# Pooling the second batch's keys: uncast pixels, row sums by GpSimd, two chunks per job, and three more GELU chunks for VectorE

## The chip, the cores and the metric

The kernel runs on one core of one Trainium2 chip. The metric is the time of one execution on the device in microseconds (us), the median of three runs. The profile is one execution taken by the hardware profiler; its times are counted from the start of its span.

## What is computed

Attention over pooled keys, followed by a feed-forward layer with a quick GELU. There are 4 batches of 12288 queries with 128 channels, 49152 rows in all; the keys are a 384 x 32 image of 128 channels per batch, pooled 4 x 4 to 768 keys.

```python
# q (4, 12288, 128), kv (4, 384, 32, 128), w_sr (128, 128)
kv_pool = kv.reshape(B, H // 4, 4, W // 4, 4, C).mean(axis=(2, 4))
k = v = kv_pool.reshape(B, -1, C) @ w_sr
s = (q @ k.transpose(0, 2, 1)) / sqrt(C)
x = softmax(s) @ v                       # (49152, 128)
h = x @ w_in                             # w_in (128, 2048)
out = (h / (1 + exp(-1.702 * h))) @ w_out
```

## The kernel before, in words

**Stages.** The rows are cut into 96 groups of 512 (`NG`), 24 to a batch. Work is done in two rounds of 48 groups (`R = 2`): attention for a round, then the feed-forward layer for it. The unit is a chunk: 512 rows against 128 keys (six to a group, `JC`) or against 128 of the 2048 hidden channels (16 to a group, `FCH`). A fill is TensorE's first matmul of up to three chunks into three of the eight PSUM banks (`fill_attn` L337, `fill_moe` L584), followed by one ScalarE activation of 128x1536 that reads them and writes weights to the buffer `ag`, which has room for 102 chunks. Two sets of three banks take turns; the other two banks are for everything else (`acc`). A drain is the second matmul, from `ag`: four of 129 columns for each attention chunk (`drain_attn` L344), one of 512 for each feed-forward chunk (`drain_moe` L590). After an attention drain VectorE divides by the sums and writes rows to `x` (L376, L379). These are put away in HBM (`put_away` L489) and brought back transposed (`bring_back` L496), as the first matmul of the feed-forward layer wants them. After a feed-forward drain VectorE transposes the group's result (L607), and SyncE's queue writes it out.

**The order.** There is no scheduler at run time. A planner at the end of the kernel (L783 to L851) walks through the fills, and between two of them puts drains, small jobs (`extras`) and steps for VectorE, by a model of the time in units of one 512-column matmul. `FIXED` and `CHUNK` are the model of an activation, `COST` and `COPY` that of the small jobs, and `RECIPROCAL` that of a reciprocal of 128x256 on VectorE. What comes out is one fixed row of instructions per engine, which the engines run in order, held up only by semaphores. `background(i)` (L517) starts loads and small jobs when the fill of group i is placed.

**The keys.** Batch 0 and batch 1 use `load_chunk` (L126): one DMA of GpSimd's queue reads 128 rows of 16 pixels as fp32 and writes them as bf16 into a slice of `x` that is free then. `pool_chunk` (L133) sums with TensorE: for each of four windows, four matmuls with the stationary operand a pixel row block and the moving operand `sum4` (128x32), accumulated over the four pixels, 16 matmuls in all, and one copy by VectorE. `key_and_value` (L157) then makes keys and values of the chunk with two matmuls of 128 columns and two copies. For batch 1 the loads are started at groups 10 and 12, three each; pooling and keys run at groups 15 to 20 and 16 to 21. Group 24 is the first that needs batch 1's keys. Batches 2 and 3 are pooled by accumulating DMAs (`add_kv` L168) and are not touched here.

**The queries.** `cast_q` (L207) writes a slice of four groups to HBM as bf16 (GpSimd's queue), and `load_qT` (L212) brings it back transposed on SyncE's queue. `CAST` and `TURN` say at which group.

**Gates.** GpSimd's and SyncE's queues would run far ahead. `gate` (L506) has VectorE write one element, and GpSimd write it again, so that GpSimd's next DMA is held until VectorE has come that far. For SyncE a write into the target by VectorE does the same (L214).

**Chunks made by VectorE.** Some exponentials (`rolling`, `early`) and 14 GELU chunks (`lent` L322: the last chunk of every third group from 52 on) are computed by VectorE instead of ScalarE, in a row of elementwise steps (`early_exp` L416, `lent_gelu` L438). The result goes to `aside`, which has room for three.

Of the kernel before, what the change touches and what calls it, by code (L numbers as in the profile page):

```python
# [24 lines left out]
def kernel(  # L25
    ctx, tc, q, kv, w_sr, moe_w_in, moe_w_out, out,
):
    nc = tc.nc
    B, N, C = q.shape
    _, H, W, _ = kv.shape  # L30
    r = 4
# [101 lines left out]
    def pool_chunk(b, jc):  # L133
# [7 lines left out]
        pTs[b, jc] = kvtmp.tile([128, 128], BF, name="pTc", bufs=2)  # L141
        nc.vector.tensor_copy(pTs[b, jc], ps[:, 0:128])

    def key_chunk(b, jc):
# [10 lines left out]
        vs[b, jc] = True  # L155

    def key_and_value(b, jc):  # L157
        if (b, jc) == (1, 0):
            new_keys(b)
        ps = acc()  # L160
        nc.tensor.matmul(ps[:, 0:128], w_sr_sb, pTs[b, jc], start=True, stop=True)
        nc.tensor.matmul(ps[:, 128:256], pTs.pop((b, jc)), w_sr_sb, start=True, stop=True)
# [156 lines left out]

    early = range(NG // R, NG // R + EARLY)  # L320
    rolling = [(i, JC - 1) for i in [*range(38, NG // R, 6), *range(57, 90, 6)]]
    lent = [(g, FCH - 1) for g in range(52, 94, 3)]  # L322
    aside = agpool.tile([128, K, 512], BF, name="aside")

    def weights(c):
# [161 lines left out]
    PART, FIRST = 24, 3  # L487

    def put_away(n, m):  # L489
        size = PART // 2 if n == 0 and m > FIRST else PART  # L490
        for o in range(m * PART, m * PART + PART, size):
            lo = n * XS * SG + o * T
            nc.sync.dma_start(out=x_bf[lo:lo + size * T, :].rearrange("(k p) c -> p k c", p=T),
                              in_=x[:, o * T:(o + size) * T].rearrange("p (k c) -> p k c", k=size))
# [11 lines left out]
    def gate():  # L506

        one = gate_tile[:, gates[0] % 8:gates[0] % 8 + 1]
        gates[0] += 1
        nc.vector.memset(one, 0.0)  # L510
        nc.gpsimd.memset(one, 0.0)  # L511

    TURN = {6: 3, 7: 4, 8: 5, 20: 6, 21: 7, 22: 8, 30: 9, 32: 10, 35: 11, 40: 12}
    CAST = {0: [5], 13: [6], 14: [7], 15: [8], 25: [9, 10], 26: [11, 12]}
    CAST_MOE = {20: 13, 21: 14, 22: 15, 23: 16, 33: 17, 34: 18, 35: 19, 36: 20, 37: 21, 38: 22, 39: 23}

    def background(i):  # L517

        first_round = i < GB * 2
        s = TURN.get(i, NS) if first_round else i // 4 + 3 if i % 4 == 0 else NS  # L520
        if s < NS:
            load_qT(s)
        if i in CAST:
            gate()
            for s in CAST[i]:
                cast_q(s)
        if i in (10, 12):
            gate()
            for jc in range(i % 10 * 3 // 2, i % 10 * 3 // 2 + 3):
# [9 lines left out]
        if i == 27:  # L539
            gate()  # L540
            nc.gpsimd.dma_start(out=w_in_sb, in_=moe_w_in)
        if i == 28:
            gate()
            nc.gpsimd.dma_start(out=w_out_sb, in_=moe_w_out.rearrange("(o p) c -> p o c", p=128))

# [155 lines left out]
    def prepare(p):  # L701

        nonlocal now
        kind, part = seq[p]
        for i, jc in part:
            if (kind, i) not in begun:
                begun.add((kind, i))
                (background if kind == "a" else background_moe)(i)
            while kind == "a" and ((key_and_value, i // GB, jc) in extras or (transpose_q, i) in extras):
# [24 lines left out]


    FIXED, CHUNK, SWITCH, HANDOVER, EVACUATE = 0.295, 1.978, 6.0, 1.0, 4.5
    COST = {pool_chunk: (1.9, 2.6), key_chunk: (0.3, 2.4), value_chunk: (0.3, 2.4),
            transpose_q: (1.05, 4.2), early_fill: (1.0, 5.5), key_and_value: (0.55, 3.5),
            transpose_pooled: (0.9, 3.6), make_k: (0.8, 3.2), make_v: (0.8, 3.7)}
    COPY = {pool_chunk: 1.5, key_chunk: 1.5, value_chunk: 1.5, key_and_value: 2.8, transpose_q: 3.2}  # L740
    SMALL = 0.26
    RECIPROCAL = 10.5
    PAUSE = 4.0
    end, extra_at = [], 0.0
    source, dve = None, 0.0
# [137 lines left out]
```

The softmax here doesn't subtract the row's maximum and nothing guards it: scores larger than these inputs give would overflow.

## Time and profile before

The time is 951.16 us (950.90 to 951.42); the profiled execution has a span of 949.0 us.

| engine | busy us | share of the span | instructions |
|---|---|---|---|
| TensorE matmul (PE) | 941.5 | 99% | 6314 |
| VectorE (DVE) | 536.8 | 57% | 1037 |
| ScalarE (ACT) | 933.9 | 98% | 708 |
| GpSimd (POOL) | 67.0 | 7% | 115 |

The costliest groups of instructions, by line:

| line | what | times | busy us | mean ns |
|---|---|---|---|---|
| L588 | ACT, GELU of three chunks | 510 | 682.2 | 1507 |
| L586 | PE, feed-forward fill, 512 columns | 1522 | 411.7 | 379 |
| L596 | PE, feed-forward drain, 512 columns | 1506 | 407.8 | 379 |
| L342 | ACT, exponential of three chunks | 192 | 245.8 | 1439 |
| L353 | PE, attention drain, 129 columns | 2272 | 163.7 | 220 |
| L340 | PE, attention fill, 512 columns | 544 | 148.7 | 379 |
| L139 | PE, pooling, 32 columns (batches 0 and 1) | 192 | small | 177 |
| L463 | DVE, half a reciprocal of a GELU chunk | 28 | 47.6 | 1726 |

How to read it: a matmul's 379 ns is its own way through the array; the next one starts long before it ends, so means do not add up to the span, and how closely starts follow each other tells more. The stages, from the windows: attention of the first round up to about 142 us, feed-forward to 487, attention of the second round to 604, feed-forward to the end. L139, L161 and L162 name the pooling and key matmuls of both batch 0 (up to 25 us) and batch 1 (from 52.8 us on).

### The profile page before, as it was taken

Reading aid. Unit: us, or ns where it says so; the run is one execution under the profiler, and the core shown is the slowest. Engines: PE = TensorE matmul, PEld = TensorE weight load, DVE = VectorE, ACT = ScalarE, POOL = GpSimd, SP = SyncE. Lnnn points to the kernel's source line nnn. Section 1 sums busy time; section 2 is a strip of 40 time slices with the busy share of each in tenths; the row PEclk is TensorE's granted clock in tenths of the full one; section 3 lists DMA queues with packets and bytes.
Section 4 is the critical chain, followed back from the end, with each engine's and each line's share of the span. In section 5 each row is a group of like instructions: output and inputs, shape, how many; then the busy total and the mean of one; then the engine's idle time right before and its main releaser. Section 6 shows DMA issues by size and latency. Waiting matters only on the chain.

```text
span 949.0 us, 15424 instructions
## 1 busy us (share of the span) xinstructions
PE 941.5 (99%) x6314; PEld 503.1 (53%) x6314; DVE 536.8 (57%) x1037; ACT 933.9 (98%) x708; POOL 67.0 (7%) x115
## 2 busy tenths in 40 slices
PE   8999999999999999999999999999999999999998
PEld 4677776444444444454446777754444444444444
DVE  5643553102477777778655765365666665566631
ACT  5999999999999999999999999999999999999998
POOL 4101001330000232000000000000000000000000
PEclk9999999999999999999999999999999999999999
DMA  9999922999867799865335583552222222222222
GB/s 182 203 181 193 214 57 42 157 127 170 162 132 113 116 147 125 123 103 78 65 55 112 133 160 77 134 122 35 44 34 45 34 46 34 45 33 45 34 45 45
DMA packets 372871, 94.93 MB, mean 100 GB/s; under 512 B 346736, under 2 KB 370416, under 8 KB 372464
## 3 DMA queue, kind: packets, MB, share of 16 engines
q1 hardware_dynamic: 343872, 61.31, 36.5%
q0 software_dynamic: 28656, 32.51, 22.6%
q8 instruction: 49, 0.80, 0.4%
q14 instruction: 22, 0.18, 0.1%
q10 hardware_dynamic: 272, 0.13, 0.0%
HBM read 52.49 MB, written 48.76 MB: 107 GB/s over the span
## 4 chain that ended last, share of the span: by engine, by line
ACT 88%; PE 9%; DMA 2%; issue 0%; DVE 0%; POOL 0%; POOLq 0%
ACT ag L588 71%; ACT ag L342 17%; PE banks L340 4%; PE banks L353 3%; DMA x<-in_kv_dram 1%; DMA qT<-q_bf 1%; PE banks L139 0%; PE banks L586 0%; PE banks L624 0%; ACT L588 0%; PE banks L596 0%; PE banks L233 0%; ACT L342 0%; DVE kT L163 0%; POOL x L222 0%
## 5 line engine op out<-in xcount | busy, mean ns | idle before, releaser
L588 ACT ACTIVATE ag<-banks 128x1536 bf16<-128x1536 f32 (+1 forms) x510 | 682.2, 1507 | 0.0
L586 PE MATMUL banks<-x,w_in_sb 128*128 128x512 bf16 x1522 | 411.7, 379 | 0.1
L596 PE MATMUL banks<-ag,w_out_sb 128*128 128x512 bf16 x1506 | 407.8, 379 | 0.0
L342 ACT ACTIVATE ag<-banks 128x1536 bf16<-128x1536 f32 (+2 forms) x192 | 245.8, 1439 | 3.7 <-PE banks L340 3.3
L596 PEld LDWEIGHTS <-w_out_sb 128*128 128x128 bf16 x1520 | 148.5, 98 | 178.0 <-issue 0.9
L586 PEld LDWEIGHTS <-w_in_sb 128*128 128x128 bf16 x1522 | 147.3, 98 | 170.4 <-issue 1.1
L607 DVE STREAM_TRANSPOSE o_sb<-banks 128x512 f32<-128x512 f32 x95 | 67.9, 715 | 210.7 <-PE banks L596 199.9
L353 PEld LDWEIGHTS <-ag 128*128 128x128 bf16 x2272 | 146.1, 98 | 46.4 <-issue 0.6
L353 PE MATMUL banks<-v,ag 128*128 128x129 bf16 x2272 | 163.7, 220 | 0.1
L340 PE MATMUL banks<-qT,kT 128*128 128x512 bf16 x544 | 148.7, 379 | 1.6 <-DVE kT L163 1.0
L432 DVE SCALAR_TENSOR_TENSOR ea<-ea,eb 128x512 f32<-128x512 f32 x128 | 87.8, 686 | 3.2
L376 DVE RECIPROCAL rec<-banks 128x3 f32<-128x3 f32 x124 | 22.2, 179 | 96.0 <-PE banks L353 96.0
L379 DVE TENSOR_TENSOR x<-banks,rec 128x384 bf16<-128x384 f32 x124 | 69.1, 557 | 4.3
L340 PEld LDWEIGHTS <-kT 128*128 128x128 bf16 x544 | 46.3, 98 | 26.6 <-DVE kT L163 1.7
L463 DVE RECIPROCAL eb<-ea 128x256 f32<-128x256 f32 x28 | 47.6, 1726 | 0.5
L173 POOL DMA_DIRECT2D kvs<-in_kv_dram x32 | 40.4, 1315 | 20.8 <-DMA kvs<-in_kv_dram 17.8
L421 DVE TENSOR_SCALAR ea<-banks 128x512 f32<-128x512 f32 x32 | 22.1, 692 | 32.6 <-PE banks L405 32.4
L456 DVE SCALAR_TENSOR_TENSOR ea<-ea,eb 128x512 f32<-128x512 f32 x56 | 38.3, 685 | 1.6
L511 POOL MEMSET gate_tile<- 1x1 f32 x37 | 3.9, 105 | 323.1 <-DVE gate_tile L510 323.1
L427 DVE SCALAR_TENSOR_TENSOR eb<-eb,ea 128x512 f32<-128x512 f32 x32 | 22.1, 690 | 0.9
L443 DVE TENSOR_SCALAR qT<-banks 128x512 f32<-128x512 f32 x14 | 9.7, 692 | 17.2 <-PE banks L399 16.9
L434 DVE SCALAR_TENSOR_TENSOR ag<-ea,ee 128x512 bf16<-128x512 f32 x24 | 16.5, 688 | 0.7
(84 smaller groups left out, 267.6 us busy)
## 6 DMA issues: line engine op xcount, KB each, us to landing
out_dram<-o_sb SPq DMA_DIRECT2D x380, 64.0 KB, 2.0
kvs<-in_kv_dram POOLq DMA_DIRECT2D x32, 384.0 KB, 6.5
q_bf<-in_q_dram POOLq DMA_DIRECT2D x21, 512.0 KB, 6.9
x_bf<-x SPq DMA_DIRECT2D x12, 768.0 KB, 5.8
x<-in_kv_dram POOLq DMA_DIRECT2D x12, 512.0 KB, 10.5
x_bf<-x SPq DMA_DIRECT2D x8, 384.0 KB, 4.5
x<-in_q_dram POOLq DMA_DIRECT2D x5, 256.0 KB, 15.2
w_in_sb<-in_moe_w_in_dram POOLq DMA_DIRECT2D x1, 512.0 KB, 9.6
```

The costliest lines, as they stand in the source:

```text
L173: nc.gpsimd.dma_start(out=kv_sums[b][:, i2], in_=kv_p[b, i, w, :, i2], **({"accum_op": ADD} if n else {}))
L340: nc.tensor.matmul(ps[:, k, :], kTs[i // GB][:, jc * 128:(jc + 1) * 128], rhs, start=True, stop=True)
L342: nc.scalar.activation(place([("a",) + c for c in chunks]), ps, AF.Exp, scale=scale)
L353: nc.tensor.matmul(av_of[u][:, k * (C + 1):(k + 1) * (C + 1)], weights(("a", i, jc))[:, o:o + T], vs[i // GB][:, jc, 0:C + 1], start=(jc = ...
L379: nc.vector.tensor_tensor(to, ps[:, :, 0:C], rec.unsqueeze(2).broadcast_to([128, TS, C]), MUL)
L432: nc.vector.scalar_tensor_tensor(a, a, COEFFS[k], b, ADD, MUL)
L456: nc.vector.scalar_tensor_tensor(a, a, COEFFS[k], b, ADD, MUL)
L463: nc.vector.reciprocal(b[:, m:m + 256], a[:, m:m + 256])
L586: nc.tensor.matmul(ps[:, k, :], w_in_sb[:, fc * 128:(fc + 1) * 128], x[:, g % (4 * XS) * G:(g % (4 * XS) + 1) * G], start=True, stop=True)
L588: nc.scalar.activation(place([("m",) + c for c in chunks]), ps, AF.Gelu_apprx_sigmoid)
L596: nc.tensor.matmul(o_of[g], w_out_sb[:, fc, :], weights(("m", g, fc)), start=(fc == 0), stop=(fc == FCH - 1))
L607: nc.vector.transpose(o_sb, o_of.pop(g))
```

## The change

Batch 1's pixels are no longer cast on the way. `load_pixels` loads one chunk at a time on SyncE's queue as fp32, twice the room in SBUF, so that three chunks fit and the fourth waits for the first to be summed. GpSimd, which has little to do, adds the four pixels of a window in three `tensor_tensor` instructions per chunk (`sum_pixels`); the third writes bf16 into half of a buffer from the pool of the output tiles. TensorE then needs one matmul per window instead of four, and two chunks are one job (`pool_sums`, `key_pair`): eight matmuls of 32 columns and one copy, then one matmul of 256 columns, two of 128, and two copies. It is meant to take matmuls and copies away and to give the idle engine work.

With it come: 17 GELU chunks for VectorE instead of 14 (the last chunk of groups 52, 54, 57, 59 and so on); casts and loads of the queries moved (slices 6 to 8 are cast three groups later, behind most of GpSimd's adds; slices 9 to 12 and the weights one group earlier); two more blocks of `x` put away in halves; two gates fewer on GpSimd's queue, while only the first three of the six loads on SyncE's queue have a holding write; and planner costs for the new jobs, with 8.2 instead of 10.5 for a reciprocal.

```diff
+    def load_pixels(jc):
+        a, ch = divmod(jc, HC)
+        o = (XS - JC) * SG + jc % 3 * 2 * SG
+        t = x[:, o:o + 2 * SG].bitcast(F32)
+        if jc < 3:
+            nc.vector.memset(t[:, 0:1], 0.0)
+        nc.sync.dma_start(out=t, in_=kv_r[1, a, ch])
+        kv_tiles[1, jc] = t.rearrange("p (wp w1 c) -> p w1 wp c", w1=r, c=C)
+    def sum_pixels(jc):
+        t = kv_tiles.pop((1, jc))
+        if jc % 2 == 0:
+            held[jc // 2] = opool.tile([128, 512], F32, name="o_sb").bitcast(BF)
+        sums[jc] = held[jc // 2][:, jc % 2 * 512:jc % 2 * 512 + 512].rearrange("p (wp c) -> p wp c", c=C)
+        nc.gpsimd.tensor_tensor(t[:, 0], t[:, 0], t[:, 1], ADD)
+        nc.gpsimd.tensor_tensor(t[:, 2], t[:, 2], t[:, 3], ADD)
+        nc.gpsimd.tensor_tensor(sums[jc], t[:, 0], t[:, 2], ADD)
+    def pool_sums(b, jc):
+        ps = acc()
+        for k in range(2):
+            for wp in range(4):
+                o = k * 128 + 32 * wp
+                nc.tensor.matmul(ps[:, o:o + 32], sums[jc + k][:, wp, :], sum4, start=True, stop=True)
+        pTs[b, jc] = kvtmp.tile([128, 256], BF, name="pTp")
+        nc.vector.tensor_copy(pTs[b, jc], ps[:, 0:256])
+    def key_pair(b, jc):
...
+        nc.tensor.matmul(ps[:, 0:256], w_sr_sb, pT, start=True, stop=True)
+        for k in range(2):
+            nc.tensor.matmul(ps[:, 256 + k * 128:384 + k * 128], pT[:, k * 128:(k + 1) * 128], w_sr_sb,
+                             start=True, stop=True)
+        nc.vector.tensor_copy(kTs[b][:, jc * 128:(jc + 2) * 128], ps[:, 0:256])
+        nc.vector.tensor_copy(vs[b][:, jc:jc + 2, 0:C], ps[:, 256:512].rearrange("p (k c) -> p k c", k=2))
...
-    lent = [(g, FCH - 1) for g in range(52, 94, 3)]
+    lent = [(g, FCH - 1) for g in range(52, 94) if g % 5 in (2, 4)]
...
-        size = PART // 2 if n == 0 and m > FIRST else PART
+        size = PART // 2 if n == 0 and m > 1 else PART
...
-    TURN = {6: 3, 7: 4, 8: 5, 20: 6, 21: 7, 22: 8, 30: 9, 32: 10, 35: 11, 40: 12}
-    CAST = {0: [5], 13: [6], 14: [7], 15: [8], 25: [9, 10], 26: [11, 12]}
+    TURN = {6: 3, 7: 4, 8: 5, 20: 6, 21: 7, 22: 8, 29: 9, 31: 10, 35: 11, 40: 12}
+    CAST = {0: [5], 16: [6], 17: [7], 18: [8], 24: [9, 10], 25: [11, 12]}
...
-        if i in (10, 12):
-            gate()
-            for jc in range(i % 10 * 3 // 2, i % 10 * 3 // 2 + 3):
-                load_chunk(1, jc)
-        if 0 <= i - 16 < JC:
-            extras.append((key_and_value, 1, i - 16))
-        if 0 <= i - 15 < JC:
-            extras.append((pool_chunk, 1, i - 15))
+        if 10 <= i < 10 + JC:
+            if i > 10:
+                sum_pixels(i - 11)
+            for jc in range(3) if i == 10 else [i - 8] if i < 14 and i > 10 else []:
+                load_pixels(jc)
+        if i == 10 + JC:
+            sum_pixels(JC - 1)
+        if i in (15, 18, 21):
+            extras.append((pool_sums, 1, (i - 15) // 3 * 2))
+        if i in (16, 19, 22):
+            extras.append((key_pair, 1, (i - 16) // 3 * 2))
...
-    RECIPROCAL = 10.5
+    RECIPROCAL = 8.2
```

More of the change, by code (lines that the diff above doesn't have):

```diff
@@ L142, in pool_chunk @@
         nc.vector.tensor_copy(pTs[b, jc], ps[:, 0:128])
+    held, sums = {}, {}
+    def load_pixels(jc):
[23 more added lines that the diff above has]
+    def key_pair(b, jc):
+        if jc == 0:
+            new_keys(b)
+        ps = acc()
+        pT = pTs.pop((b, jc))
+        nc.tensor.matmul(ps[:, 0:256], w_sr_sb, pT, start=True, stop=True)
[4 more added lines that the diff above has]
+        nc.vector.tensor_copy(vs[b][:, jc:jc + 2, 0:C], ps[:, 256:512].rearrange("p (k c) -> p k c", k=2))
+        vs[b, jc] = vs[b, jc + 1] = True
     def key_chunk(b, jc):
@@ L157, in key_and_value @@
     def key_and_value(b, jc):
-        if (b, jc) == (1, 0):
-            new_keys(b)
         ps = acc()
@@ L538, in background @@
             bring_back(0, (i - 31) // 5)
-        if i == 27:
+        if i == 26:
             gate()
             nc.gpsimd.dma_start(out=w_in_sb, in_=moe_w_in)
-        if i == 28:
+        if i == 27:
             gate()
@@ L708, in prepare @@
                 (background if kind == "a" else background_moe)(i)
-            while kind == "a" and ((key_and_value, i // GB, jc) in extras or (transpose_q, i) in extras):
+            while kind == "a" and ((key_pair, i // GB, jc // 2 * 2) in extras or (transpose_q, i) in extras):
                 f, *args = extras.pop(0)
@@ L736 @@
     FIXED, CHUNK, SWITCH, HANDOVER, EVACUATE = 0.295, 1.978, 6.0, 1.0, 4.5
-    COST = {pool_chunk: (1.9, 2.6), key_chunk: (0.3, 2.4), value_chunk: (0.3, 2.4),
+    COST = {pool_chunk: (1.9, 2.6), pool_sums: (1.1, 3.2), key_pair: (1.1, 5.0), key_chunk: (0.3, 2.4), value_chunk: (0.3, 2.4),
             transpose_q: (1.05, 4.2), early_fill: (1.0, 5.5), key_and_value: (0.55, 3.5),
             transpose_pooled: (0.9, 3.6), make_k: (0.8, 3.2), make_v: (0.8, 3.7)}
-    COPY = {pool_chunk: 1.5, key_chunk: 1.5, value_chunk: 1.5, key_and_value: 2.8, transpose_q: 3.2}
+    COPY = {pool_chunk: 1.5, pool_sums: 2.1, key_pair: 4.2, key_chunk: 1.5, value_chunk: 1.5, key_and_value: 2.8, transpose_q: 3.2}
     SMALL = 0.26
-    RECIPROCAL = 10.5
+    RECIPROCAL = 8.2
     PAUSE = 4.0
```

## The prediction

> **What bounds the kernel now.** I read the page first, its chain of waits next, then the windows and the timeline.
>
> ```profile
> PE 941.5 (99%) x6314; PEld 503.1 (53%) x6314; DVE 536.8 (57%) x1037; ACT 933.9 (98%) x708; POOL 67.0 (7%) x115
> ...
> ACT 88%; PE 9%; DMA 2%; issue 0%; DVE 0%; POOL 0%; POOLq 0%
> ```
>
> TensorE (PE) and ScalarE (ACT) are both full, and the chain names ACT. Since each hands work to the other all the time, the chain can walk back through either. So I ask each engine for its smallest pitch. First PE, by windows:
>
> ```profile
> core 0: us, PE busy (x) PEld busy (x) DVE busy (x) ACT busy (x) POOL busy (x), PEclk, DMA share, GB/s
> 45.00:75.00 30.00, 29.90 (x394) 21.91 (x392) 12.84 (x49) 29.89 (x23) 3.34 (x9) 1.00 0.94 177
> 160.00:260.00 100.00, 100.00 (x481) 45.89 (x479) 21.61 (x44) 100.00 (x75) 19.13 (x21) 1.00 1.00 149
> 660.00:900.00 240.00, 240.00 (x1113) 108.77 (x1112) 148.89 (x209) 240.00 (x179) 0.00 (x0) 1.00 0.25 39
> ```
>
> From 660 to 900 us, 1113 matmuls, all 512 columns wide, take 240 us: 215.6 ns each. The timeline has three of them start 0.65 us before the next three (660.18, 660.82), 215 ns each. That is the pitch of matmuls in one unbroken row, so PE has no hole there. Now ACT, in the end of the first attention stage:
>
> ```profile
> 128.66 13.60 ACT L342 ACTIVATE ag<-banks 128x1536 bf16<-128x1536 f32 x10
> ```
> ```profile
> 139.31 2.95 ACT L342 ACTIVATE ag<-banks 128x1536 bf16<-128x1536 f32 x2
> ```
>
> The ninth starts 10.65 us after the first: 1.331 us a piece, the floor of a 1536-wide activation (its mean of 1507 ns includes overlap with the one before). The chain has ACT L588 x28 in 37.6 us from 885.5 to 923.2, a pitch of 1.345. So late in the run PE runs at its floor and ACT 1% above its own. PE is the narrower one. Added up by kind from the program's order, at 216 ns (512 columns), 57 (129), 56 (128) and 25 (32), PE's work is 933 us of 949; most of the rest lies before 40 us. ACT from 13.1 us, at its floor of 1.331 (0.90 for 1024), needs 921 us and takes 931.
>
> **What the skill says.** Perfetto Trace Analysis, "Identifying the Most-Contended Engine", calls matmul busy time a poor measure, since matmuls are pipelined: the trace agrees (a row of 379 ns every 216), which is why I use pitches. TensorE: Matmul & The Clock Gate, "Back-to-back issue gap", gives N/2.4 + 2.5 ns, 215.8 for 512 columns, and about 25 ns up to 64 columns: the trace shows 215.6 and 25. It also says that 512-column streams sustain 131 ns; no such pitch stands here, and the measurement decides. SBUF, "two separate sides", says that GpSimd and VectorE share a port pair, locked when VectorE has two SBUF inputs or a two-port mode; in 46 to 69 us VectorE's long work (L379, the copies L142 to L164) reads PSUM, so I expect no lock. No GpSimd add is in the trace of before.
>
> **The change part by part.**
>
> Pooling matmuls. Before, each of six chunks of batch 1 has 16 matmuls of 32 columns, and two key and value matmuls:
>
> ```profile
> 52.79 0.55 PE L139 MATMUL banks<-sum,x 128*128 128x32 bf16 x16
> ...
> 53.19 0.38 PE L340 MATMUL banks<-qT,kT 128*128 128x512 bf16 x1
> ```
> ```profile
> 55.22 0.22 PE L162 MATMUL banks<-w_sr_sb,pTc 128*128 128x128 bf16 x1
> ...
> 55.54 0.27 PE L353 MATMUL banks<-v,ag 128*128 128x129 bf16 x2
> ```
>
> 53.19 - 52.79 = 0.40 us, or 25 ns each. 96 go and 24 come: 72 x 25 ns = 1.8 us off PE. Keys and values: six times 0.11 (58.08 to 58.20) become three times 0.22, nothing. All this is PE work on a full PE, so it counts whole. I add 0.25 us for the one hole after L162 at 55.2 ("issue", 0.23), which a job with half as many copies may not have.
>
> GELU chunks. Three more go from ACT to VectorE. PE's two matmuls for each stay. On ACT one 1536-wide activation goes, 1.33 us. In built order PE work ahead of the n-th fill is the same to 0.2 us in both programs for most of the run (the planner puts drains where PE was freed); the gain appears at the end, where the last fill stands 1.4 us earlier, with 0.4 us less PE work behind it. So 1.33 and 1.8 are not to be added: together 1.8. VectorE pays 11.0 us a chunk (154 us for the 14 in 620 to 940, from its groups), 33 us. It is busy 149 of 240 us there: hidden, if no chunk comes late (below).
>
> Transposes of q. The casts and loads for groups 36 on go one group (2.66 us) earlier. They end this wait, 0.2 us of PE:
>
> ```profile
> 100.49 0.10 PEld L405 LDWEIGHTS <-kT 128*128 128x128 bf16 x1 [0.22 <-DMA qT<-q_bf]
> ```
>
> Casts of slices 6 to 8 go three groups later, 8 us. They took about 14 us in a full queue, and their transposed loads are issued only at 66, 69 and 73 us for groups from 24 (77 us): hidden. The halved writes of x and fewer gates lie beside PE's queue: nothing.
>
> The new wait: pixels, adds, pooling. PE now waits for GpSimd. Behind the waiting weight load stand all later fills and drains, so each us there is a us of the total, once ACT has emptied its two fills. The loads go out on SyncE after its three transposes, which hold it from 30.00 to 39.88 us. The first cast load, issued at 39.00, landed 7.0 us later at 46.0. In 46 to 56 us the queues write 213 GB/s in bf16, so 0.52 MB, one chunk, every 2.46 us, which reads twice that. I take the same rate for uncast pixels: 46.0, 48.5, 51.0. An add of 512 fp32: GPSIMD Engine Reference, "Elementwise", has 4497 ns for 2048, hence an estimate of 1.12 us. Lower end 0.8; upper 1.5, if strides or locks cost. Three and their waits: 3.5 us a chunk. So chunk 1 is summed at 46.0 + 7.0 = 53.0, where PE's old pool job stood at 52.8 (the new one stands at the same place in built order): a stall of 0.3. The pairs at groups 18 and 21 (60.7 and 68.7 us) need chunk 3 at 60.0 and chunk 5 at 67.0: in time. Later loads wait for the sums of three chunks before (49.5, 53, 56.5) and land in about 4 us, ahead of their adds.
>
> The same page, "Instruction dispatch", has some 6 us for the first call after a library is loaded. The built program does reload a library on GpSimd ahead of the first add; it waits for nothing and stands behind the cast issued at 18.4 us, when GpSimd has nothing to do until 38 us. I take it as hidden.
>
> Sum: -1.8 - 0.25 - 0.2 + 0.3 = -1.95. 951.16 becomes 949.2; I say **949.1**.
>
> **The rivals.**
> 1. GpSimd is late (slower). With 1.5 us an add, 4.6 a chunk: chunk 1 at 55.2 stalls 2.3, chunk 3 at 64.4 another 1.3, chunk 5 at 73.6 another 1.4; 5.0 - 2.25 gives 953.9. If the library is paid at the first add, about 6.3 - 2.25 gives 955.2. For it: pairs have hardly a microsecond in hand. Against: the early place of the reload.
> 2. ACT binds, as the chain says. Then freed PE time is waste, and only the one activation counts: 951.16 - 1.35 = 949.8. For it: in the first attention stage ACT is at its floor too. Against: the 1.345 pitch later.
> 3. Lent chunks come late. They now stand two and three groups apart, not three. Two groups of 6.8 us are 13.6; a lent chunk and two transposes of 0.71 are 12.4. Half a microsecond at each of the seven or so close pairs: +3.5 - 2.0 gives 952.7. Against: before, VectorE idles 2.3 us inside a lent chunk (653.6 to 655.9), as the planner priced reciprocals at 10.5 for the 8.0 they take.
> 4. More holes close than I count, with no stall: 948.0.
>
> **How the numbers follow.** The forecast 0.60, three quarters of it below 949.26, the 0.2% line; rival 2 0.17, rival 1 0.11, rival 4 0.07, rival 3 0.05. Faster 0.45 + 0.07 = 0.52; same 0.15 + 0.17 = 0.32; slower 0.16. The range, 947.8 to 953.2, takes in rivals 2 and 3 and adds up to 1.35 us, and leaves out the worst of rival 1.
>
> **What would show it.** Right: 24 pooling matmuls at 25 ns; adds near 1.1 us, the first at 46 us; under 0.5 us of waiting for GpSimd at the pooling weight load; PE's pitch still 215.6 ns after 660; L342 and L588 ends 1 to 2 us earlier. Wrong: a PE wait of several us at 53 to 55 us; adds of 1.5 us; pixels landing after 48 us; a wait of PE for the set-aside tile after 620 us.

## The result and the profile after

The changed kernel takes 960.5 us (958.87 to 961.57, five runs) against 951.12 us for the kernel before: a ratio of 1.0096, with a 95% interval of 1.0081 to 1.011. The change makes the kernel 9.4 us slower. The forecast was 949.1 us, with a range of 947.8 to 953.2. The profiled execution took 958.87 us, with a span of 956.8 us against 949.0.

The page of the kernel after, its engines, granted clock and chain:

```profile
PE 941.9 (98%) x6239; PEld 502.5 (53%) x6239; DVE 567.4 (59%) x1074; ACT 933.3 (98%) x707; POOL 85.5 (9%) x125
...
PEclk9998999999999999999999999999999999999999
...
PE 48%; ACT 46%; DMA 4%; POOL 1%; issue 0%; DVE 0%; SPq 0%; POOLq 0%
```

75 PE instructions fewer stand in the trace and PE is as busy as before: 0.4 us more, in a span 7.8 us longer. The clock has a slice of 8 that was 9 before. The chain now has 4% of DMA and 1% of GpSimd. The waits of TensorE in the kernel after name the places (line waited at, what for: us in total, times, longest):

```profile
PE banks L383 <- DMA qT<-q_bf: 5.8, 1, 5.8
PE banks L139 <- DMA x<-in_kv_dram: 1.5, 2, 0.8
PE banks L448 <- DMA qT<-q_bf: 1.4, 1, 1.4
...
PE banks L172 <- POOL o_sb L164: 0.2, 1, 0.2
```

The pooling matmul (L172) hardly waits for GpSimd. Two waits for transposed queries stand out: 5.8 us by an attention fill (L383), which is new, and 1.4 us by a fill for VectorE (L448), where the weight load of the kernel before waited 0.2 us. The wait at L139 stood before too. Now the windows: three of the kernel after, and below them the one of the kernel before that answers to the second:

```profile
core 0: us, PE busy (x) PEld busy (x) DVE busy (x) ACT busy (x) POOL busy (x), PEclk, DMA share, GB/s
60.00:76.00 16.00, 16.00 (x188) 11.53 (x186) 7.38 (x24) 15.98 (x13) 9.79 (x14) 1.00 0.62 133
76.00:88.00 12.00, 6.18 (x51) 4.33 (x49) 1.48 (x5) 4.57 (x5) 1.13 (x4) 0.72 1.14 204
...
660.00:900.00 240.00, 240.00 (x1113) 108.68 (x1112) 174.20 (x243) 240.00 (x180) 0.00 (x0) 1.00 0.26 39
```
```profile
76.00:88.00 12.00, 12.00 (x140) 8.81 (x138) 4.42 (x16) 12.00 (x10) 3.87 (x10) 1.00 1.01 209
```

From 660 us PE's pitch is what it was, 240/1113 = 215.6 ns. Nearly all is lost in 76 to 88 us, where PE does 51 matmuls (140 in the kernel before) at a mean clock of 0.72, and in a smaller piece at 107 us. The timeline of PE around the first hole:

```profile
76.42 0.59 PE L383 MATMUL banks<-qT,kT 128*128 128x512 bf16 x2
82.84 0.59 PE L383 MATMUL banks<-qT,kT 128*128 128x512 bf16 x1 [5.82 <-DMA qT<-q_bf]
```

That is the fill of group 24, the first that needs slice 6 of the queries. The records of the clock say 0.50 from 80.0 to 86.8 us, and the windows about these times show it:

```profile
80.00:82.80 2.80, 0.00 (x0) 0.00 (x0) 0.00 (x0) 0.00 (x0) 0.00 (x0) 0.50 0.89 187
82.80:86.80 4.00, 3.96 (x26) 2.86 (x26) 0.74 (x2) 2.21 (x2) 0.00 (x0) 0.50 0.69 154
86.80:90.00 3.20, 3.20 (x37) 2.32 (x36) 1.39 (x5) 2.87 (x3) 1.05 (x3) 1.00 1.14 241
```

A wait can also be counted as the time by which two starts of PE lie apart beyond their usual pitch; it comes out about 0.16 us longer than the idle time in the lists, 6.0 for 5.8 here. Most waits below are counted so. Summed over the whole run, this gives 11.45 us before and 20.74 after: 6.2 more in 60 to 80 us (the hole counts where it begins), 1.8 in 80 to 100 (half clock) and 1.3 in 100 to 120 (the second wait). These 9.3 less the 1.8 of matmuls removed make 7.5 of the 7.8 us between the spans.

Why was slice 6 late? GpSimd's timeline in the kernel after, and below it the same casts in the kernel before:

```profile
45.55 1.27 POOL L162 TENSOR_TENSOR x<-x 128x512 f32<-128x512 f32 x1 [26.94 <-DMA x<-in_kv_dram]
...
63.31 1.27 POOL L164 TENSOR_TENSOR o_sb<-x 128x512 bf16<-128x512 f32 x1
64.52 0.09 POOL L554 MEMSET gate_tile<- 1x1 f32 x1
64.56 0.52 POOL L252 DMA_DIRECT2D q_bf<-in_q_dram  x1
65.10 1.28 POOL L162 TENSOR_TENSOR x<-x 128x512 f32<-128x512 f32 x1
...
68.92 0.51 POOL L252 DMA_DIRECT2D q_bf<-in_q_dram  x1
```
```profile
47.41 0.51 POOL L209 DMA_DIRECT2D q_bf<-in_q_dram  x1
...
49.08 0.49 POOL L209 DMA_DIRECT2D q_bf<-in_q_dram  x1
...
53.06 0.49 POOL L209 DMA_DIRECT2D q_bf<-in_q_dram  x1
```

The adds run back to back from 45.55 us. The cast of slice 6 (L252) stands in the same row of instructions, behind the sums of the first five chunks, and is issued at 64.56 instead of 47.41 us; those of slices 7 and 8 at 68.92 and 69.46. The casts land at 69.82, 74.54 and 76.98 us. SyncE's transposed load of slice 6, after and before:

```profile
69.96 6.90 SPq L258 DMA_TRANSPOSE qT<-q_bf  x1
```
```profile
66.03 1.83 SPq L215 DMA_TRANSPOSE qT<-q_bf  x1
```

It starts 3.9 us later, which alone would be harmless (it landed at 70.11 before, and is needed at 76.6). But now the casts of slices 7 and 8 are under way beside it. Its issue takes 6.90 us in place of 1.83, and ends at 76.86, just before the cast of slice 8 lands. The rest of its way takes 5.94 us instead of 2.25, with the casts of slices 9 and 10, issued from 76.22 us, beside it (79.00 before). It lands 12.84 us after its start, at 82.80.

### The profile page after: what moved, and what is told of

It reads as the page before. It is cut to its first block, busy times and chain, and to the rows that moved or that the text cites. A ratio compares the mean times of both kernels' runs of the same rounds, so it can differ in the third digit from the quotient of the medians.

```text
span 956.8 us, 15342 instructions
## 1 busy us (share of the span) xinstructions
PE 941.9 (98%) x6239; PEld 502.5 (53%) x6239; DVE 567.4 (59%) x1074; ACT 933.3 (98%) x707; POOL 85.5 (9%) x125
## 4 chain that ended last, share of the span: by engine, by line
PE 48%; ACT 46%; DMA 4%; POOL 1%; issue 0%; DVE 0%; SPq 0%; POOLq 0%
ACT ag L634 34%; PE banks L632 18%; PE banks L642 17%; ACT ag L385 12%; PE banks L396 6%; PE banks L383 5%; DMA qT<-q_bf 3%; DMA x<-in_kv_dram 1%; PE banks L448 1%; PE banks L670 0%; POOL o_sb L164 0%; POOL x L162 0%; POOL x L163 0%; PE banks L139 0%; PE banks L276 0%
## 5 line engine op out<-in xcount | busy, mean ns | idle before, releaser
L383 PE MATMUL banks<-qT,kT 128*128 128x512 bf16 x544 | 149.8, 381 | 7.4 <-DMA qT<-q_bf 5.8
L475 DVE SCALAR_TENSOR_TENSOR ea<-ea,eb 128x512 f32<-128x512 f32 x128 | 87.5, 684 | 3.7 <-DVE ea L475 0.6
L383 PEld LDWEIGHTS <-kT 128*128 128x128 bf16 x544 | 46.4, 98 | 26.0 <-DVE kT L206 1.7
L506 DVE RECIPROCAL eb<-ea 128x256 f32<-128x256 f32 x34 | 57.8, 1724 | 0.5
L499 DVE SCALAR_TENSOR_TENSOR ea<-ea,eb 128x512 f32<-128x512 f32 x68 | 46.6, 686 | 2.0
L486 DVE TENSOR_SCALAR qT<-banks 128x512 f32<-128x512 f32 x17 | 11.8, 692 | 22.9 <-PE banks L442 22.6
```

The costliest lines, as they stand in the source:

```text
L383: nc.tensor.matmul(ps[:, k, :], kTs[i // GB][:, jc * 128:(jc + 1) * 128], rhs, start=True, stop=True)
L475: nc.vector.scalar_tensor_tensor(a, a, COEFFS[k], b, ADD, MUL)
L499: nc.vector.scalar_tensor_tensor(a, a, COEFFS[k], b, ADD, MUL)
L506: nc.vector.reciprocal(b[:, m:m + 256], a[:, m:m + 256])
```

## The experiments

Times are medians; each ratio is to the kernel before on the same chip, with its 95% interval; it is made from all runs and can differ a little from that of the medians. "After" and "before" in a diff's first line say which kernel was edited. The theory after the look at the two traces: the casts come late because they stand behind the adds on GpSimd's queue, and their load then meets other casts. The rivals: the later group alone does it; the queues are simply overloaded by fp32 pixels; or, on the side of the gain, ScalarE sets the pace and the three lent chunks are all there is to win.

### The place of the casts

```diff
# after
-    CAST = {..., 16: [6], 17: [7], 18: [8], ...}
+    CAST = {..., 13: [6], 14: [7], 15: [8], ...}
```

> The changed kernel with one edit: slices 6 to 8 are cast at groups 13 to 15 again, so that their DMAs stand on GpSimd's queue behind the sums of chunks 0 to 3 and not behind those of 3 to 5. Theory A (GpSimd's own order: the cast of slice 6 could be issued only at 64.6 us, when the sum of chunk 4 was over, and the transposed load for group 24 came 6 us late): the casts go out at about 53, 57 and 61 us, TensorE's wait of 5.8 us before group 24 and the half clock after it go, the second wait of 1.6 us near 108 us shrinks or goes, and the time is 949 to 950 us. Rival B (the DMA queues carry 3 MB more of uncast pixels and the transposed load is slow for that, 12.8 us where it took 4 to 8): the wait stays at 3 us or more, and the time is 955 us or above. Rival C (the loss is the three more lent chunks or the new jobs): 959 us.

956.2 us, 1.0051 (1.0038 to 1.0064). The wait at group 24 is gone, but only 4.3 of 9.4 us come back, and none of the expectations is met in full. A new wait stands in its place, as the waits of weight loads and GpSimd's timeline show:

```profile
PEld L172 <- POOL o_sb L164: 3.9, 2, 3.5
```
```profile
69.64 1.26 POOL L162 TENSOR_TENSOR x<-x 128x512 f32<-128x512 f32 x1 [3.50 <-DMA x<-in_kv_dram]
```

The casts, issued at 53.03, 57.39 and 61.75, now meet the pixels: the last chunk's load, issued at 57.44, lands at 69.57 us, 12 us instead of 5, so GpSimd sums it late, the third pooling job waits 3.5 us, and the clock is at half from 73.7 to 77.1 us. The rival of the overloaded queues has a part in it: pixels are slow with casts beside them.

```diff
# before
-    CAST = {..., 13: [6], 14: [7], 15: [8], ...}
+    CAST = {..., 16: [6], 17: [7], 18: [8], ...}
```

> The kernel before with one edit: slices 6 to 8 are cast at groups 16 to 18, as in the changed kernel; no adds, pixels cast on the way. Theory A: GpSimd's queue is free then, the casts are issued at about 55, 58 and 61 us, land by 68 us, no wait for q at group 24, time 950.5 to 951.5 us. Rival D (the later cast by itself is too late for the load at group 20): TensorE waits 2 us or more for the transposed slice, 954 us or above.

951.23 us, 1.0 (0.9992 to 1.0008). The same later groups cost nothing without the adds: the casts land by 69.31 us, and the loads start at 66.13, 69.43 and 72.67. The rival of the later group falls.

```diff
# after
-        nc.gpsimd.tensor_tensor(t[:, 0], t[:, 0], t[:, 1], ADD)
-        nc.gpsimd.tensor_tensor(t[:, 2], t[:, 2], t[:, 3], ADD)
```

> The changed kernel without the first two of the three adds per chunk, so that only two of each window's four pixels are summed; all loads, casts, jobs and their places stay. GpSimd then needs 1.3 us a chunk instead of 3.8. Theory A (the casts of slices 6 to 8 were late because they stand behind the adds): they are issued where the groups come, at about 55 to 61 us, the 6 us wait before group 24 and the half clock go, 949 to 951 us. Rival F (the wait comes from the cast's later group or from the pixel bytes, and not from GpSimd's time): 955 us or more.

950.72 us (949.55 to 955.26), 1.0005 (0.9995 to 1.0014). This kernel leaves out half of each window's sum. With one add in place of three the casts are issued at 58.85, 61.35 and 61.89 us, the three transposed loads take 9.1 us together, and the wait at group 24 is gone, with every DMA of the change in place (the last three pixel loads start 2 to 5 us earlier, as they wait for sums). That supports the theory: GpSimd's time ahead of the casts causes the first wait. The second is still there: 1.49 us at 99.3 us.

### The half clock

```diff
# after
+        if (24, 0) in part and kind == "a":
+            ps = acc()
+            for _ in range(24):
+                nc.tensor.matmul(ps[:32, :], ones, ...)   # 512 columns, not read
```

> The changed kernel with 24 matmuls of 512 columns on constants put on TensorE's queue ahead of the fill that holds group 24's first chunk; their results are read by nobody. They take 24 x 0.216 = 5.2 us, in the time of the 6 us wait. If the granted clock of one half from 80.0 to 86.8 us follows from TensorE standing idle and costs about 2 us on top of the wait: no half clock there, 957 to 958.5 us (2 us less than the changed kernel), though 5 us of work were added. If the half clock has another cause or costs nothing: the changed kernel's 960.5, or more.

957.54 us, 1.007 (1.0057 to 1.0083). The matmuls end at 82 us, so the load has time to land, and nothing but the idling has been taken away. The window of this run that answers to the one of 0.72 above:

```profile
76.00:88.00 12.00, 11.71 (x98) 6.81 (x96) 2.09 (x8) 6.38 (x6) 2.11 (x6) 1.00 1.10 196
```

The clock stays at 1.00. From 1.0096 to 1.007 is 2.5 us: about the price of the half clock after the wait, on top of the wait. It is no closer than that: the two intervals just touch, the profile of after has 1.8 us, and the second wait is 3.2 us in this run's profile instead of 1.6. After that second wait the clock stayed at 1.00.

### Other places for pixels and casts

```diff
# after
-        if 10 <= i < 10 + JC:       # pixels and sums from group 10
+        if 7 <= i < 7 + JC:         # from group 7; casts at 10, 11, 12; TURN {6: 3, 8: 4, 10: 5}
```

> The changed kernel with its data moved so that nobody queues: the first three pixel loads are started at group 7 instead of 10, between the transposed loads for groups 12 and 16, when the DMA queues are nearly idle; the sums follow from there, and slices 6 to 8 are cast at groups 10 to 12. Work per engine is that of the changed kernel. Theory A (GpSimd's order and the crowded queues of 45 to 70 us are the loss; the freed TensorE work is real): no wait for GpSimd at the three pooling jobs, none for q at group 24, 949 to 950.5 us; the wait near 106 us may stay, 0 to 1.5 us. Rival E (the change loses elsewhere): 954 us or more.

963.21 us, 1.0124 (1.011 to 1.0138): the expectation failed. SyncE's timeline shows the transposed loads of slices 4 and 5, which now share the queues with the pixels:

```profile
36.50 10.03 SPq L258 DMA_TRANSPOSE qT<-q_bf  x1
46.63 1.75 SPq L153 DMA_DIRECT2D x<-in_kv_dram  x2
48.55 12.13 SPq L258 DMA_TRANSPOSE qT<-q_bf  x1
```

10 and 12 us each, and each holds the pixels behind it on SyncE's queue. PE waits 10.1 us for slice 5 at 65.4, and the clock is at half for 10.2 us.

Two variants were run along with it. One puts the casts and loads of slices 9 to 12 and the weights where the kernel before has them:

```diff
# the kernel of e5_pixels_early
-    TURN = {..., 29: 9, 31: 10, ...}; CAST = {..., 24: [9, 10], 25: [11, 12]}; weights at 26, 27
+    TURN = {..., 30: 9, 32: 10, ...}; CAST = {..., 25: [9, 10], 26: [11, 12]}; weights at 27, 28
```

> The kernel with early pixels, and slices 9 to 12, the two weight loads and the transposed loads of slices 9 and 10 at the groups of the kernel before (one group later). If the move by one group is what makes the second wait, near 106 us (0.2 us in the kernel before, 1.2 to 3.2 in the kernels with the move): that wait falls to 0.2 to 0.6 us, and the time is 0.5 to 1.5 us below that of the kernel with early pixels alone. If not: the same within 0.5 us.

963.55 us, 1.0126 (1.0113 to 1.0139), and the other has 14 lent chunks:

```diff
# the kernel of e5_pixels_early
-    lent = [(g, FCH - 1) for g in range(52, 94) if g % 5 in (2, 4)]; RECIPROCAL = 8.2
+    lent = [(g, FCH - 1) for g in range(52, 94, 3)]; RECIPROCAL = 10.5
```

> The kernel with early pixels, but with the 14 GELU chunks and the price of 10.5 of the kernel before: the pooling part of the change alone. If TensorE's work sets the time, and the three more chunks bring nothing by themselves (951.4 us against 951.3 when added alone): equal to the kernel with early pixels within 0.6 us, near 949.5. If the freed TensorE time is only of use once ScalarE is relieved too: 0.8 to 1.5 us slower than that kernel.

965.57 us, 1.0153 (1.0125 to 1.018). The long wait, 8.7 and 13.3 us in their profiles, differs by more than these edits could do, and the single runs of the second spread from 961.53 to 971.0: both say nothing on their question.

Next, the casts ahead of all sums, pooling and key jobs one group later, and the later casts, loads and weights as before:

```diff
# after
-    CAST = {..., 16: [6], 17: [7], 18: [8], ...};  pooling at 15, 18, 21, keys at 16, 19, 22
+    CAST = {..., 10: [6, 7, 8], ...};              pooling at 16, 19, 22, keys at 17, 20, 23
```

> The changed kernel with another order of its transfers: slices 6 to 8 are cast at group 10, ahead of the pixels and the adds on GpSimd's queue, the three pooling jobs and the three key jobs stand one group later, and slices 9 to 12, their loads and the weights are at the groups of the kernel before. Theory A, with what the run with early pixels showed (a transposed load issued while casts or pixels are under way holds SyncE's queue for 7 to 12 us instead of 2 to 4): the transposed loads at 66 to 72 us find quiet queues, the pixels land about 2 us later than in the changed kernel, waits for GpSimd at the pooling jobs 0 to 1 us each, no wait for q, 948.8 to 950.5 us. If the order of the transfers isn't the cause: 954 us or more.

961.74 us, 1.0107 (1.0093 to 1.0122): the expectation failed. Three casts together take the queues, the first pixels land at 52.85 instead of 45.4 us, and PE waits 1.65 and 3.66 us for GpSimd, with 6.8 us of half clock after it. The second wait is there too, 2.7 us. The same with the casts one after another at 11, 12 and 13:

```diff
# the kernel of e9_casts_first
-    CAST = {..., 10: [6, 7, 8], ...}
+    CAST = {..., 11: [6], 12: [7], 13: [8], ...}
```

> As the run with casts first, but slices 6 to 8 are cast at groups 11 to 13, between the sums of the first chunks. Theory A: the casts run beside the pixels of chunks 2 to 4, the last pixels land by 66 us, the transposed loads are quiet or nearly so; waits for GpSimd of 1 to 3 us in all; 950 to 952.5 us. If the pixels are held up by the casts as in the run with casts at 13 to 15 (12 us for the last chunk, 3.6 us of waiting): 953 us or more.

955.34 us (952.54 to 958.97), 1.0042 (1.0027 to 1.0057), slower than expected. The profiled execution is one of the faster ones, 953.37 us. In it, waits for GpSimd are under 0.2 us, and the transposed loads of slices 6 to 8 are issued quietly, in under 2.1 us each. What is left there is the second wait. TensorE's wait in this run, and the windows about it:

```profile
PE banks L448 <- DMA qT<-q_bf: 2.2, 1, 2.2
```
```profile
98.00:101.70 3.70, 1.62 (x16) 0.94 (x15) 0.74 (x2) 3.25 (x3) 0.00 (x0) 1.00 1.18 161
101.70:105.10 3.40, 3.24 (x19) 2.15 (x20) 1.13 (x3) 0.34 (x1) 0.00 (x0) 0.50 1.24 235
```

A wait of 2.35 us brings 3.4 us at half clock behind it.

### The second wait

In the kernel after, slice 9's transposed load is issued at 97.50 and lands at 109.41 us; the cast loads of `w_in` and `w_out`, issued at 90.42 and 93.75, are under way until 101.78 and 109.23. The change had moved all this one group earlier. First that move alone:

```diff
# before
-    TURN = {..., 30: 9, 32: 10, ...}; CAST = {..., 25: [9, 10], 26: [11, 12]}; weights at 27, 28
+    TURN = {..., 29: 9, 31: 10, ...}; CAST = {..., 24: [9, 10], 25: [11, 12]}; weights at 26, 27
```

> The kernel before with one part of the change: slices 9 to 12, the weights and the transposed loads of slices 9 and 10 one group earlier. If that move makes the second wait (the load of slice 9 issued at 89 to 90 us, while the casts of slice 12 and of the weights are under way until 99 us, where it is issued at 93 us before): a wait of 1 to 2 us near 100 us instead of 0.2, 952 to 953 us. If it relieves the wait, as I forecast: 951.1 us.

951.87 us (950.48 to 954.69), 1.0002 (0.9994 to 1.001): neither gain nor loss that can be measured, and in the profile the wait is 1.36 us, where the kernel before has 0.2. Then the weights out of the way. They are first used from about 142 us on:

```diff
# the kernel of e10_casts_between
-        if i == 27:      # w_in;  28: w_out
+        if i == 42:      # w_in;  43: w_out
```

> As the run with casts between, but the two weight loads are started at groups 42 and 43 instead of 27 and 28; they are needed only at 141 us, and the queues are empty from 128. Theory A in full (both waits are transposed loads of q that come late because other transfers hold the queues): the load of slice 9, issued at 93 us, lands by 98 us, the wait near 100 us falls from 2.4 us to under 0.3, the half clock after it goes, no other wait of TensorE over 0.5 us; 948.5 to 950 us, so 1.3 to 2.8 us below the kernel before: the freed pooling work. If the freed work isn't on the path: 951 us or more.

951.36 us, 1.0 (0.9992 to 1.0009): 4 us less than with the weights early, but not the 948.5 to 950 that were expected. The load of slice 9 is issued in 1.84 us instead of 4.67, and the wait is gone:

```profile
94.15 1.84 SPq L258 DMA_TRANSPOSE qT<-q_bf  x1
```

The same in the kernel after:

```diff
# after
-        if i == 26:      # w_in;  27: w_out
+        if i == 42:      # w_in;  43: w_out
```

> The changed kernel with one edit: the weight loads at groups 42 and 43. The first wait (6 us at group 24, half clock after it) stays, the second (1.6 us near 108 us) goes: 957.5 to 959.5 us against 960.5. If the second wait has another cause: 960 us or more.

956.99 us, 1.0056 (1.0044 to 1.0069): by the medians 3.5 us of 9.4 come back, more than expected. In its profile the second wait is gone and the first is 3.0 us instead of 6.0. But the weights' loads, issued at 90.42 us in the kernel after, come behind the first wait, and this profile is of an execution of 954.87 us, the fastest of five; the other four took 956.88 to 957.28. So the shorter first wait may be chance, and it does not explain the median. And in the kernel before:

```diff
# before
-        if i == 27:      # w_in;  28: w_out
+        if i == 42:      # w_in;  43: w_out
```

> The kernel before with the loads of w_in and w_out started at groups 42 and 43 instead of 27 and 28, nothing else. It has only the 0.2 us wait for transposed queries to lose: 951.0 to 951.3, same as before. If the weights' loads cost the kernel before something that its waits do not show, it comes out 0.5 us or more below.

950.55 us, 0.9993 (0.9984 to 1.0001). Perhaps half a microsecond is won; the interval still includes nothing.

### What the freed work is worth

```diff
# before
-    lent = [(g, FCH - 1) for g in range(52, 94, 3)]; RECIPROCAL = 10.5
+    lent = [(g, FCH - 1) for g in range(52, 94) if g % 5 in (2, 4)]; RECIPROCAL = 8.2
```

> The kernel before with 17 GELU chunks by VectorE instead of 14 and a planner's price of 8.2 for a reciprocal; nothing else. Theory of the prediction (the last fill comes one activation, 1.4 us, earlier; TensorE's total work stays): 949.7 to 951.1 us, between a gain of one activation and nothing. Rival C (chunks by VectorE come late where they stand two groups apart): waits of TensorE for the set-aside tile, 952 us or more.

951.36 us, 1.0004 (0.9996 to 1.0012): three more chunks for VectorE bring nothing to the kernel before. That ScalarE alone sets the pace is refuted. The chain of the page of this run has turned from 88% ACT to

```profile
PE 97%; DMA 2%; DVE 0%; ACT 0%; POOL 0%; issue 0%; POOLq 0%
```

ScalarE's last row of GELU ends at 943.03 us instead of 944.10, but TensorE's last row of matmuls at 946.3 us, where it was 945.8 before: the drains left over for the end take as long as ever. The reverse, fewer lent chunks on the best order found so far:

```diff
# the kernel of e12_weights_late
-    lent = [(g, FCH - 1) for g in range(52, 94) if g % 5 in (2, 4)]; RECIPROCAL = 8.2
+    lent = [(g, FCH - 1) for g in range(52, 94, 3)]; RECIPROCAL = 10.5
```

> As the run with weights late, but with the 14 GELU chunks and the price of 10.5 of the kernel before. If TensorE's work sets the time (three more chunks alone brought 951.4 against 951.3): the same as that run within 0.7 us. If ScalarE sets it once TensorE is relieved: 1.0 to 1.5 us slower than that run.

952.14 us, 1.001 (1.0001 to 1.0019), but with a wait of 2.5 us for GpSimd and 3.4 us of half clock in its profile, so it could not be read. Hence first a kernel in which nothing takes the freed work back:

```diff
# the kernel of e6_one_add
-        if i == 26:      # w_in;  27: w_out
+        if i == 42:      # w_in;  43: w_out
```

> The kernel after without the first two of the three adds of each chunk (the sums hold only two of the four pixels of a window: work is left out), and with the loads of w_in and w_out started at groups 42 and 43. Both waits for transposed queries should then be gone and GpSimd should be in time, so this run shows what the freed TensorE work is worth when nothing takes it back. If the 1.8 us of pooling matmuls are worth their time: 1.8 us under the kernel before, 949.3, range 948.5 to 950.3. If freed TensorE time does not count (another limit lies right behind it): 950.8 to 951.4, as in the run with one add alone.

948.88 us, 0.9974 (0.9964 to 0.9985). There is no wait for queries or for GpSimd, and the kernel, which leaves out half of each window's sum, is 2.2 us faster than before. Perhaps 0.5 of it is the weights'; with that taken off, 1.7 of the forecast's 1.95 us were there to be had. Then a whole computation with less work for GpSimd. The room for its second sums is the weights' own, which is free until they are loaded:

```diff
# after, with the weights at 42 and 43
-        nc.gpsimd.tensor_tensor(t[:, 0], t[:, 0], t[:, 1], ADD)
-        nc.gpsimd.tensor_tensor(t[:, 2], t[:, 2], t[:, 3], ADD)
-        nc.gpsimd.tensor_tensor(sums[jc], t[:, 0], t[:, 2], ADD)
+        sums[jc] = sums[jc], <512 columns of w_in_sb or w_out_sb>
+        nc.gpsimd.tensor_tensor(sums[jc][0], t[:, 0], t[:, 1], ADD)
+        nc.gpsimd.tensor_tensor(sums[jc][1], t[:, 2], t[:, 3], ADD)
...
-                nc.tensor.matmul(ps[:, o:o + 32], sums[jc + k][:, wp, :], sum4, start=True, stop=True)
+                for h in range(2):
+                    nc.tensor.matmul(ps[:, o:o + 32], sums[jc + k][h][:, wp, :], sum4, start=h == 0, stop=h == 1)
```

> The whole computation. GpSimd makes two bf16 sums of two pixels each per chunk (two adds instead of three, 2.5 us instead of 3.8), the second sums lie in the tiles of w_in and w_out, which are loaded only at groups 42 and 43; TensorE adds the two sums, 48 pooling matmuls of 32 columns instead of 24 (96 in the kernel before). If GpSimd's time ahead of the casts is what cost the time: the cast of slice 6 is issued at about 58 us, no wait for transposed queries over 0.3 us, and the freed 48 x 25 ns = 1.2 us plus what the later weights gave alone (0.5) stay: 949.5, range 948.8 to 950.3. If two adds are still too many: a wait of 1 to 3 us at group 24 and 951 to 954.

949.35 us (949.17 to 950.1), 0.9979 (0.997 to 0.9989): faster than both kernels. GpSimd's and SyncE's timelines:

```profile
57.81 1.27 POOL L166 TENSOR_TENSOR w_out_sb<-x 128x512 bf16<-128x512 f32 x1
59.02 0.09 POOL L557 MEMSET gate_tile<- 1x1 f32 x1
59.06 0.52 POOL L255 DMA_DIRECT2D q_bf<-in_q_dram  x1
```
```profile
65.33 9.83 SPq L261 DMA_TRANSPOSE qT<-q_bf  x3
```

The cast goes out at 59.06 us, 5.5 us earlier than in the kernel after, and three transposed loads take 9.83 us, against 6.90 for one. The window that was half empty is full again, at full clock:

```profile
76.00:88.00 12.00, 12.00 (x140) 8.81 (x138) 4.43 (x13) 11.99 (x10) 2.10 (x6) 1.00 1.09 231
```

Last, the lent chunks once more on this base:

```diff
# the kernel of e17_two_adds
-    lent = [(g, FCH - 1) for g in range(52, 94) if g % 5 in (2, 4)]; RECIPROCAL = 8.2
+    lent = [(g, FCH - 1) for g in range(52, 94, 3)]; RECIPROCAL = 10.5
```

> The version with two adds per chunk and later weights, with 14 GELU chunks on VectorE and 10.5 for a reciprocal as in the kernel before, instead of 17 and 8.2. If TensorE sets the pace and three more lent chunks bring nothing: 949.35 within 0.3. If ScalarE comes next once TensorE has 1.2 us less to do: up to 1.2 us more, 950 to 950.6.

950.58 us, 0.9996 (0.9988 to 1.0004): 1.2 us more than with 17. The intervals of the two ratios just touch; the single runs, on two chips whose kernels before differ by 0.2 us, do not overlap (949.17 to 950.1 with 17, 950.48 to 950.85 with 14). ScalarE's timeline in the end of the two, first with 17, then with 14:

```profile
924.73 18.24 ACT L637 ACTIVATE ag<-banks 128x1536 bf16<-128x1536 f32 x16
```
```profile
923.92 20.89 ACT L637 ACTIVATE ag<-banks 128x1536 bf16<-128x1536 f32 x18
```

The last GELU ends at 942.97 with 17 and at 944.81 with 14; before it was 944.10. Lent chunks alone bring 0, freed TensorE work with later weights about 0.4 (no more than later weights do by themselves), all three together 1.8. So each of the two engines stands right behind the other.

The lent chunks with later weights and the old pooling were not run, so that the 1.8 us could in part be theirs. The traces speak against it. All of TensorE's matmuls, added up at their usual pitch (an estimate from the starts), make 932.9 us in the kernel before and with lent chunks alone, and 931.6 in both runs with two adds: only the pooling takes work off TensorE. And with 14 lent chunks TensorE waits 0.8 us for ScalarE at 911 to 913 us, with 17 no such wait is listed.

## Why the prediction was wrong

**The step that failed.** It is the sentence "Casts of slices 6 to 8 go three groups later, 8 us. They took about 14 us in a full queue, and their transposed loads are issued only at 66, 69 and 73 us for groups from 24 (77 us): hidden." It counts groups, and it does not ask what stands ahead of the casts on GpSimd's own queue, though the section on the change says "behind most of GpSimd's adds" and the section on the adds had put those very adds there, to 67.0 us. From the prediction's own numbers the sum of the fifth chunk ends at 46.0 + 5 x 3.5 = 63.5 us, and the cast of slice 6 comes behind it; it came at 64.56, as a chunk's three adds took 3.8 us. Later groups alone cost nothing (951.23), one add in place of three took the wait away (950.72).

**A transfer's length taken as fixed.** The same sentence reads the loads' start, not their length. The start moved only from 66.03 to 69.96 us, 6.7 us ahead of the need. The load's issue, 1.83 us before, took 6.90 next to casts that used to be over. The Trainium skill has the ground for it in DMA: Bandwidth & Descriptors, "Issuing engines are not separate DMA queues": all issuers share the same 16 engines and interleave. It adds that initiating a DMA is usually short beside the DMA itself; here the issue was 6.90 of 12.84 us, up to 12.13 in the run with early pixels, and the measurement decides. That the transfers beside it cause the length is read from how the two go together in these runs; the load in an otherwise equal queue without casts wasn't tried by itself. They go together closely: the long issues mostly end just before another transfer lands. In the kernel after those of slices 6 and 7 end at 76.86 and 84.79 us, and casts land at 76.98 and 84.97; in the run with early pixels one ends at 60.68, and pixels land at 60.73.

**The clock.** The forecast let a stall cost its own length. After the wait of 6.0 us the granted clock was 0.50 for 6.8 us, and the unread matmuls took back some 2 us. The Trainium skill, TensorE: Matmul & The Clock Gate, "The HAM clock gate", says just that: half clock after an idle window of some 3.4 us, full clock after about as long of work. The records of after agree (half clock begins 3.4 us after the last matmul before the wait starts, at 76.64), but elsewhere a wait of 2.35 us was enough for 3.4 us of half clock, and one of 3.2 us, in the run with the filled wait, brought none. Prices for rivals 1 and 3 lacked this.

**Slices 9 to 12 and the weights one group earlier.** "They end this wait, 0.2 us of PE" had the wrong sign in the profile: 1.58 us at 107.66 us, for the load of slice 9 met the cast loads of the weights. The move alone made 0.2 into 1.36 us; with the weights moved away the wait is gone.

**What was right.** The pixels were forecast for 46.0, 48.5 and 51.0 us and landed at 45.38, 47.87 and 50.35. The stall at the first pooling job was to be 0.3 and was 0.39 us; the two later jobs were in time. The adds take 1.27 us, inside the bounds of 0.8 and 1.5 and above the 1.12 chosen. The library reloads out of sight: the first add begins 0.17 us after its pixels land. No lent chunk came late. PE's pitch from 660 us is unchanged. The sum of -1.95 us was right as a sum of these parts: with GpSimd's time and the weights' loads out of the way the kernel gains 2.2 us, perhaps 0.5 of it from the weights. Against the forecast's reason for it, though, the activation removed is not merely swallowed by the 1.8: in the version with two adds, without the three lent chunks 1.2 of its 1.8 us go.

**The rivals.** Rival 1 had the right engine and the wrong victim: GpSimd was late for the casts, not for the pooling. Its 953.9 also needed adds of 1.5 us. (The range was said to leave out only the worst of rival 1, but 953.9, its milder case, lies above 953.2 as well.) Rival 2 (ScalarE binds, 949.8) is refuted for the kernel before by 951.36: ScalarE is only the next to bind once TensorE has less to do. Rivals 3 and 4 didn't occur.

**What stays open.** Why the median of the kernel after falls by 3.5 us when only the weights go later; how much of the first wait is due to the casts of slices 9 and 10, which the change had also moved; and whether the order with casts between the sums (951.36, 949.45 to 953.88) is held up by its waits for GpSimd, 1.1 us in its profile, or by something else.

## What to carry to other kernels

Work given to an idle engine also stands in its queue: list what that engine issues behind the new work, DMAs above all, and add the new work's time to each start, instead of counting the iterations by which it was moved. A transfer that had microseconds in hand has them only in the company it had; if it is moved next to others, price it at the length seen in a full queue. Reckon with half clock after a wait of TensorE of more than about two microseconds; it came after all such waits here but one. When two engines are both full, relief of one may be worth little without relief of the other, so test the parts of such a change together as well as alone.

## What the runs showed of the hardware

- A transposed load on SyncE's queue took 1.5 to 4.0 us to issue when no cast, pixel or weight load was under way. Beside such transfers it took up to 12.1 us in the run with early pixels and 17.0 in its variant with 14 lent chunks, and what stood behind it on that queue waited.
- A pixel load of 1 MB landed 2.5 us after the one before it when pixels alone ran (45.38, 47.87, 50.35 us). From issue to landing the later ones took 4.9 to 5.0 us, and one took 12.1 us with casts of queries beside it.
- TensorE's granted clock went to 0.50 after waits of 2.35 us (for 3.4 us), 6.0 us (6.8) and 10.1 us (10.2). In the traces of all runs it did so after every wait of 2.24 us or more but one of 3.2 us, and after none of 1.95 us or less. It stayed at 1.00 when unread matmuls filled the wait.
- A GpSimd add of 128x512 fp32 takes 1.27 us, with fp32 or bf16 output.
